# New DMA durations and stage priorities for the scheduler inside a two-branch attention kernel

## The chip, the cores and the metric

The kernel runs on one core of one Trainium2 chip. The metric is device time in microseconds from the first to the last instruction of the launch, as the median of several runs. The core has five instruction streams that run side by side and meet only through semaphores: TensorE (PE; its weight loads are listed apart as PEld), VectorE (DVE), ScalarE (ACT), GpSimd (POOL) and SyncE (SP). In this kernel SP does nothing but issue DMAs. The before kernel measures 364.31 us (three runs, 361.88 to 366.60); the profiled execution took 361.27 us, with a span of 359.5 us between first and last instruction.

## The reference

Two attention layers read the same input x (2048 tokens, width 640, 32 heads of 20) and their outputs are mixed by a per-token gate.

```python
# A: linear attention with a softmax feature map
q, k, v = split(x @ wqkv)                               # 32 heads of 20
phi = lambda t: concat(softmax(t @ w_phi), softmax(-(t @ w_phi)))
kv = einsum('bhsf,bhsd->bhfd', phi(k), v);  z = phi(k).sum(s)
a = ((phi(q) @ kv) / (phi(q) @ z + 1e-6)) @ wo
# B: four segments of 512 tokens: causal softmax attention inside the
#    segment plus a linear memory M, z carried over the segments
for s in range(4):
    p = softmax(q_s @ k_s.T * 20**-0.5 + causal);  dot = p @ v_s
    mem = (phi_B(q_s) @ M) / (phi_B(q_s) @ z + 1e-6)   # phi_B: t+1 if t>0 else exp(t)
    o_s = g * mem + (1 - g) * dot
    M += phi_B(k_s).T @ v_s;  z += phi_B(k_s).sum()
b = o @ wo
out = sigmoid(x . gate_w) * a + (1 - sigmoid(x . gate_w)) * b
```

## The kernel before

No order is written out by hand. The program describes some 1,490 operations as a graph (`op`, line 109, and `dma`, line 611). Each has the engines that may run it, an assumed duration, a priority `pr` (lower is sooner) and the tiles that it reads and writes. `schedule` (line 136) then plays the graph forward: at each step it takes, on every engine, the ready operation of lowest `pr` among those that could start within `DELTA` = 0.12 us of the earliest, and appends the one that starts first. For a DMA the assumed duration has two parts, `dur` (SP is occupied issuing) and `lat` (from the end of the issue to the landing). The result is one fixed list for each engine, with semaphore waits where lists depend on each other. The assumed times are used only to choose this order. On the chip every engine works through its list in that order, and an instruction that waits holds up all that stand behind it.

The names used below, with their lines:

- B works in 4 segments n of 8 steps g (four heads each), step number s = 8n + g, and this number is the common scale of all priorities. `b_step` (902) does the scores (QK, L923) in three bursts, the exponentials (L933, L952 on ACT), the causal masks (L938 on POOL) and the product with v (PV, L978 to L982). `combine` (988) divides, scales and writes `oB` on DVE, and so frees the PSUM banks of PV.
- `b_proj` (760) makes q and k (L782). Each head needs its 20 rows in its own quarter of the partitions, and 12 of the 32 rows in each quarter go elsewhere: four DMAs write them to DRAM ("relw", L790), four read them back ("relr", L793). Steps 5 to 7 of a segment need them.
- `b_mem` (830) updates the memory. It needs k with tokens on partitions, by five DMA transposes per segment ("kT", L838, tile `pk`); the first work on them is `pkt1` (L844, DVE).
- `a_k` (1052), for each of 16 token tiles t: the feature product and v (pkA and vA, L1065), exponentials, Zsum, Zrec and Anorm on DVE (L1080 to L1083), a DMA transpose of the result ("TT.t", issued through `spread`, L1097) and two adds of it into `acc` ("chain", L1090 and L1092).
- `a_kv` (1102): kv, 20 matmuls for each of two signs, once every four tiles (L1112); `a_fin` closes A's sums; `load_wo` loads the two output weights, 800 KB each ("WoA", "WoB").
- `a_q` (1155): Zq, rb, U (L1227) and the DMA transpose of the result ("oTA", L1242); `b_out` does the same for B ("oTB", L1040).
- `final` (1256): twenty matmuls per token tile against `Wo` (L1267, L1268), the eviction, and the store ("out", L1279).

PSUM has 8 banks, taken as 4 pairs; a score burst takes two pairs, so the next burst often waits for whoever must empty a pair. The constants that set the priorities stand at lines 495 to 509: `B0`, `V0`, `BN`, `VN` (projections), `KT`, `PK`, `MM` (memory), `PVP` (PV and combine), `OT`, `UO`, `AK`, `AQ`, `FI`. For example, TT and chain of tile t have priority `AK[0] + AK[1] * t`.

Of the kernel before, what the change touches and what calls it, by code (L numbers as in the profile page):

```python
# [13 lines left out]
D = 640  # L14
H = 32
DH = 20
NT = 16
NCH = 5
NG = 8
SEG = 4  # L20
LSEG = 512
HB = (0, 6, 12, 19, 24)
HEADS_OF = ((0, 6), (6, 12), (12, 19), (19, 25), (25, 31))
# [429 lines left out]
class GatedMix(Graph):  # L453
# [38 lines left out]
                if t.off < s.off + pool.size and s.off < t.off + t.size:  # L492
                    s.occ.append(t)

    B0 = (-10.0, 1.059)
    V0 = (-9.5, -0.512)
    BN = (-5.5, 0.604)
    VN = (-1.043, 0.3)
    PQ = (0.22, 1.0)
    KT = (2.0, 0.6)  # L500
    PK = (5.6, 0.3)
    MM = 6.815
    OT = (8.718, 0.2)
    PVP = (1.269, 1.394)
    FUQ = 3.0
    UO = (2.2, 0.6, 2.8)
    AK = (2.626, 1.032)
    AQ = (17.6, 4.1)
    FI = 10.953

    def memory(self):
        nc = self.nc
# [115 lines left out]
    def setup(self):  # L628
        ins = self.ins
        x2d = ins["A_x"].rearrange("b s d -> (b s) d")  # L630
        wqkv = ins["A_wqkv"]
        wsrc = lambda w: w.rearrange("(c p) n -> p c n", p=128)
        xT = self.xT
        def xload(s, pr, dur):
            sl = slice(LSEG * s, LSEG * (s + 1))
            return self.dma("sp", xT[:, :, sl], x2d[sl, :], W=[(xT, s)], pr=pr, transpose=True, name=f"x{s}", dur=dur, lat=3.0)
# [1 line left out]
        self.op("dve", 0.1, lambda e: e.memset(zf[:, :, :], 0.0), W=[(zf, "*")], pr=-60)  # L638
        self.op("act", 1.5, lambda e: e.activation(zf[:, :, :], zf[:, :, :], ACT.Exp), W=[(zf, "*")], pr=-60)
        xr = self.xr  # L640
        self.dma("sp", xr[:, :, :], x2d[0:LSEG, :].rearrange("(t p) d -> p t d", p=128), W=[(xr, "*")], pr=-60, lat=4.3, name="xr")
        for k, (st, w) in enumerate(((self.stq, "B_wq"), (self.stk, "B_wk"))):
            for h, (k0, k1) in enumerate(self.PIECES[k]):
                self.dma("sp", st[:, k0:k1, :], wsrc(ins[w])[:, k0:k1, :], W=[(st, h)], pr=-59 + 2 * k + 0.1 * h, dur=0.45, lat=5.0 + 2.6 * k + 0.25 * h, name="st")
        self.dma("sp", self.WvB[:, :, 0:D], wsrc(ins["B_wv"]), W=[(self.WvB, "w")], pr=-54, lat=8.0, name="WvB")
        self.dma("sp", self.wkT[:, :, :], wqkv[0:D, D:2 * D], W=[(self.wkT, "*")], pr=-53, dur=5.0, lat=7.0, transpose=True, name="wkT")
        self.dma("sp", self.WvA[:, :, :], wsrc(wqkv[:, 2 * D:3 * D]), W=[(self.WvA, "*")], pr=-52, lat=10.0, name="WvA")
        xload(1, -51, 4.0)
        xload(2, -50, 4.0)
        self.dma("sp", self.wqT[:, :, :], wqkv[0:D, 0:D], W=[(self.wqT, "*")], pr=-49, dur=5.0, lat=2.5, transpose=True, name="wqT")  # L650
        xload(3, -48, 4.0)
        self.dma("pool", self.WvB[:, :, D:D + 1], ins["gate_w"].rearrange("(c p o) -> p c o", p=128, o=1), W=[(self.WvB, "g")], pr=-40, lat=8.0, noncontig=True, name="gw")
        self.dma("pool", self.beta[:, :], ins["B_beta"].partition_broadcast(128), W=[(self.beta, "*")], pr=-38, lat=7.5, noncontig=True, name="beta")
        self.dma("pool", self.wphi[:, :, :], ins["A_w_phi"].rearrange("h d f -> (h d) f").rearrange("(c p) f -> p c f", p=128), W=[(self.wphi, "*")], pr=-39, lat=7.5, noncontig=True, name="wphi")
# [34 lines left out]
        for c in range(NCH):  # L689
            pt = self.pst("x0", 1)  # L690
# [7 lines left out]
        for w, st in ((0, self.stq), (1, self.stk)):  # L698
# [20 lines left out]
           W=[(Bs, "*")], pr=0)  # L719
        op("pool", 0.8, lambda e: e.affine_select(v, v, pattern=[[-1, 640]], compare_op=ALU.is_ge, fill=0.0, base=DH - 1, channel_multiplier=DH),  # L720
           W=[(Bs, "*")], pr=0)
        self.dma("sp", Bs[32:64, :, :], Bs[0:32, :, :], R=[(Bs, "*")], W=[(Bs, 1)], pr=0, name="Bsel")
        for k, (wT, Wd) in enumerate(((self.wkT, self.WkA), (self.wqT, self.WqA))):
            for ic in range(NCH):
                self.fuse(wT, Wd, ic, (0.0 if k == 0 else self.FUQ) + 0.1 * ic)
# [34 lines left out]
    def b_proj(self, n):  # L760
# [27 lines left out]
        prr = base + 5 * (self.BN[1] if n else self.B0[1])  # L788
        for i in range(4):
            self.dma("sp", scr.rearrange("(c s r) w t -> s r c (w t)", s=4, r=12)[i], qk[32 * i + DH:32 * i + 32, 0:5, :, :].rearrange("p c w t -> p c (w t)"),  # L790
                     R=[(qk, (w, c)) for w in range(2) for c in range(NCH)], W=[(sT, i)], pr=prr, nbytes=123e3, name="relw")
        for i in range(4):
            self.dma("sp", qk[32 * i:32 * i + DH, 5:8, :, :].rearrange("p c w t -> p c (w t)"), scr.rearrange("(m i d) w t -> i d m (w t)", i=4, m=3)[i],  # L793
                     R=[(sT, "*")], W=[(qk, f"r{i}")], pr=prr, nbytes=123e3, name="relr")
        for tl in range(4):
            t = 4 * n + tl
            pr = (self.V0[0] + self.V0[1] * tl) if n == 0 else 8 * n + self.VN[0] + self.VN[1] * tl
# [32 lines left out]
    def b_mem(self, n):  # L830
        if n >= SEG - 1:
            return
        qk = self.qk[n % 2]
        mp = self.pst("M", 2)
        vt = self.v1B[n % 2]
        pk = self.sbt("pk", [128, 4, D], BF16, self.p_pk)
        for c in range(NCH):
            self.dma("sp", lambda c=c: pk[:, :, 128 * c:128 * (c + 1)], qk[:, c, 1, :], R=[(qk, (1, c))],  # L838
                     W=[(pk, c)], pr=8 * n + self.KT[0] + self.KT[1] * c, transpose=True, dur=1.25, lat=1.9, name="kT")
        for tl in range(4):  # L840
            pr = 8 * n + self.PK[0] + self.PK[1] * tl
            tm = self.sbt("tmp", [128, D], BF16, self.p_tmp)
            rg = [(pk, c) for c in range(NCH)]
            self.op("dve", 0.36, lambda e, tl=tl, tm=tm: e.tensor_scalar(tm[:, :], pk[:, tl, :], 1.0, 1.0, op0=ALU.add, op1=ALU.max),  # L844
                    R=rg, W=[(tm, "*")], pr=pr, name="pkt1")
            self.op("act", d_act(D), lambda e, tl=tl: e.activation(pk[:, tl, :], pk[:, tl, :], ACT.Exp), R=[(tm, "*")],
                    W=[(pk, ("t", tl))], pr=pr, name="pkexp")
            self.op("dve", 0.56, lambda e, tl=tl, tm=tm: e.tensor_tensor(pk[:, tl, :], pk[:, tl, :], tm[:, :], ALU.min),
                    R=[(tm, "*")], W=[(pk, ("t", tl))], pr=pr, name="pkmin")
        pr = 8 * n + self.MM  # L850

        def mm(e):
            for c in range(NCH):
                b, c0 = (0, 168 * c) if c < 3 else (1, 168 * (c - 3))
                for k, h0 in enumerate((4 * c, XH[c])):
                    n4 = min(4, H - h0)
                    for tl in range(4):
                        r = e.matmul(self.pf(mp, b, c0 + 84 * k, 21 * n4), lhsT=pk[:, tl, 128 * c:128 * (c + 1)],
                                     rhs=vt[:, tl, h0:h0 + n4, :], start=(tl == 0), stop=(tl == 3))
            return r  # L860
        self.op("pe", 40 * 0.04, mm, R=[(pk, ("t", tl)) for tl in range(4)] + [(vt, tl) for tl in range(4)] + [(vt, "one")], W=[(mp, 0), (mp, 1)], pr=pr, name="Mmm")
        Mz = self.Mzb[n % 2]
        for b, c0, c1 in ((0, 0, 3), (1, 3, 5)):
            w = 168 * (c1 - c0) - (21 if c1 == 5 else 0)
            msl = self.M32[:, 168 * c0:168 * c0 + w]
            if n == 0:
                self.op("dve", d_dve(w, 1, True), lambda e, b=b, w=w, msl=msl: e.tensor_copy(msl, self.pf(mp, b, 0, w)),
                        W=[(mp, b), (self.M32, b)], pr=pr, name="Macc")
            else:
                self.op("dve", d_dve(w, 1, True), lambda e, b=b, w=w, msl=msl: e.tensor_tensor(msl, msl, self.pf(mp, b, 0, w), ALU.add),  # L870
                        W=[(mp, b), (self.M32, b)], pr=pr, name="Macc")
        self.op("dve", d_dve(819), lambda e: e.tensor_tensor(
            Mz[:, 0:819], self.M32[:, 0:819], self.Mm[:, 0:819], ALU.mult),
            R=[(self.M32, 0), (self.M32, 1), (self.Mm, "*")], W=[(Mz, "*")], pr=pr, name="Mz")
# [157 lines left out]
    def b_out(self, n):  # L1032
        oB = self.oB
        for qi in range(4):
# [2 lines left out]
            self.oTB[4 * n + qi] = oT  # L1037
            rd = [(oB, (g, qi // 2)) for g in range(NG)]
            if n < SEG - 1:
                self.dma("sp", lambda oT=oT: oT[:, :, :], lambda qi=qi: oB[:, qi, :], R=rd, W=[(oT, "*")], pr=pr, transpose=True, dur=1.28, lat=1.8, name="oTB")  # L1040
                continue
            pt = self.pst("oTB", 1)

# [52 lines left out]

    def spread(self, E, T, pr):  # L1097
        self.dma("sp", lambda: T[:, :, :], lambda: E[:, :, :].rearrange("p s n -> p (s n)"), R=[(E, 0), (E, 1)], W=[(T, 0), (T, 1)], pr=pr, transpose=True,
                 dur=1.34, lat=2.1, name="TT")
        return T  # L1100

    def a_kv(self, S):
        pr = self.AK[0] + self.AK[1] * (4 * S + 4)
        ts = [4 * S + i for i in range(4)]
        for s in range(2):
            pt = self.pst("kv", 2)

            def mm(e, s=s, pt=pt):
                for c in range(NCH):
                    b, c0 = (0, 160 * c) if c < 3 else (1, 160 * (c - 3))  # L1110
                    for k, t in enumerate(ts):
                        r = e.matmul(self.pf(pt, b, c0, 160), lhsT=self.Et[t][:, s, 128 * c:128 * (c + 1)],  # L1112
                                     rhs=self.vt[t][:, DH * HB[c]:DH * HB[c] + 160], start=(k == 0), stop=(k == 3))
                return r
            self.op("pe", 20 * 0.08, mm, R=[(self.Et[t], s) for t in ts] + [(self.vt[t], "*") for t in ts], W=[(pt, 0), (pt, 1)], pr=pr, name="kv")
            for b, c0, c1 in ((0, 0, 3), (1, 3, 5)):
# [38 lines left out]
    def a_q(self, S):  # L1155
# [57 lines left out]
        for tl in range(4):  # L1213
# [26 lines left out]
            oT = self.sbt("oTA", [128, NCH, 128], BF16, self.p_oTA)  # L1240
            if S < SEG - 1:
                self.dma("sp", lambda oT=oT: oT[:, :, :], lambda oA=oA: oA[:, :], R=[(oA, 0), (oA, 1)], W=[(oT, "*")], pr=pru + 0.5,  # L1242
                         transpose=True, dur=1.28, lat=1.8, name="oTA")
            else:
                pt = self.pst("oTA", 1)

# [9 lines left out]
    def final(self, t):  # L1256
# [19 lines left out]
            self.op("pe", d_mm(*[512, 128] * 10), part(0, 10), R=[(oA, "*"), (oB, "*"), (self.Wo, 0), (self.Wo, 1)], W=P, claim=[ob], pr=pr, name="final")  # L1276
        self.evac(640, lambda: ob[:, :], lambda: self.pf(pt, 0, 0, 640), W=[(pt, 0), (pt, 1), (ob, "*")], pr=pr, name="out_ev")
        out2d = self.out.rearrange("b s d -> (b s) d")
        self.dma("sp", out2d[128 * t:128 * (t + 1), :], lambda: ob[:, :], R=[(ob, "*")], pr=pr, nbytes=164e3, name="out")  # L1279

    def build_all(self):
        self.Et, self.vt, self.oTB, self.oTA, self.TTs, self.phiT = {}, {}, {}, {}, [], {}
# [71 lines left out]
```

## Time and profile before

| what | value |
|---|---|
| time, median of 3 (range) | 364.31 us (361.88 to 366.60) |
| profiled span, granted TensorE clock | 359.5 us, 0.957 |
| ACT, POOL busy | 262.5 us (73%), 109.6 us (30%) |
| DMA: packets, bytes | 68,823, 27.52 MB (60,400 packets under 512 B) |
| issue to landing, median: TT, kT, oTB, oTA | 3.3, 2.8, 2.7, 3.4 us |

Idle time of an engine counts only where that engine, or one that waits for it, sets the pace. So the stages have to be told apart: up to about 40 us loading and first projections, from 40 to about 200 us B's segments 0 to 2 beside A's keys, from 200 us on B's segments 2 and 3 beside A's queries and the output product, and from about 340 us the last outputs alone.

### The profile page before, as it was taken

The numbers are of one execution on the slowest core, as the hardware profiler recorded it, in microseconds if no ns is written. First come the engines' busy times: TensorE is split into PE (matmuls) and PEld (weight loads), VectorE is DVE, ScalarE is ACT, GpSimd is POOL, SyncE is SP. The second block draws the span as 40 slices with busy tenths as digits, with TensorE's granted clock in tenths as the row PEclk, the third lists the DMA queues.
The fourth block names the chain that finished last, engine by engine and source line by source line (L and its number), as shares of the span: only waits on it lengthen the run. The fifth ranks groups of instructions, "written<-read, shape, count | busy, mean of one in ns | idle before, by whom it ended". The sixth has DMA issues, their size and how long they took to land.

```text
span 359.5 us, 8970 instructions
## 1 busy us (share of the span) xinstructions
PE 313.9 (87%) x3824; PEld 180.8 (50%) x3824; DVE 244.4 (68%) x479; ACT 262.5 (73%) x362; POOL 109.6 (30%) x170
## 2 busy tenths in 40 slices
PE   3999759898999799779995899979999998888896
PEld 2454424456555444565544455545556454454663
DVE  5625557798699999899995979234782439455560
ACT  3569758894999798868995898628887779166721
POOL 7832203422223435324242323202221223131400
PEclk9999969999999999998998999989999999699699
DMA  7999741364323516742238002851014202132001
GB/s 202 246 237 184 123 82 36 57 107 88 46 38 75 90 24 91 137 69 38 38 98 178 3 2 37 122 104 52 2 38 105 64 20 17 22 57 57 2 20 55
DMA packets 68823, 27.52 MB, mean 77 GB/s; under 512 B 60400, under 2 KB 66864, under 8 KB 68784
## 3 DMA queue, kind: packets, MB, share of 16 engines
q1 hardware_dynamic: 68688, 26.92, 39.2%
q8 instruction: 30, 0.49, 0.6%
q0 software_dynamic: 96, 0.04, 0.3%
q14 instruction: 9, 0.07, 0.1%
HBM read 7.57 MB, written 4.59 MB: 34 GB/s over the span
## 4 chain that ended last, share of the span: by engine, by line
PE 45%; DVE 28%; ACT 15%; DMA 6%; SPq 2%; issue 2%; POOL 1%
PE ps L1267 11%; ACT expT L933 8%; PE ps L978 5%; PE ps L782 5%; PE ps L1166 5%; DVE E L1083 5%; DMA TT<-E 4%; DVE z L1080 4%; PE ps L923 3%; DVE acc L1092 3%; PE ps L1268 3%; PE ps L803 2%; ACT expT L952 2%; PE ps L769 2%; DVE cb L1024 2%; PE ps L1227 2%
## 5 line engine op out<-in xcount | busy, mean ns | idle before, releaser
L938 POOL TENSOR_SCALAR_AFFINE_SELECT expT<-expT 128x512 bf16<-128x512 bf16 x128 | 91.2, 714 | 226.9 <-ACT expT L933 166.3
L933 ACT ACTIVATE expT<-ps 128x1024 bf16<-128x1024 f32 x128 | 123.4, 1027 | 12.6 <-PE ps L923 12.2
L923 PE MATMUL ps<-qk 20*128 20x512 bf16 (+3 forms) x512 | 35.5, 310 | 17.3 <-DVE oB L1019 6.3
L782 PE MATMUL ps<-xT,WB 128*128 128x512 bf16 x175 | 44.4, 387 | 3.5 <-DVE oB L1019 2.0
L978 PE MATMUL ps<-v1B,expT 128*128 128x21 bf16 x1280 | 43.4, 174 | 4.0 <-POOL expT L938 1.6
L978 PEld LDWEIGHTS ps<-v1B,expT 128*128 128x128 bf16 x1280 | 39.5, 97 | 13.2 <-POOL expT L938 3.7
L752 ACT ACTIVATE out<-ps 128x640 bf16<-128x640 f32 x16 | 11.3, 703 | 37.8 <-PE ps L1268 37.8
L952 ACT ACTIVATE expT<-ps 128x1024 bf16<-128x1024 f32 x32 | 32.7, 1022 | 5.5 <-PE ps L923 5.4
L923 PEld LDWEIGHTS ps<-qk 20*128 20x128 bf16 x512 | 10.3, 92 | 42.8 <-issue 8.9
L1267 PE MATMUL ps<-Wo,oTA 128*128 128x512 bf16 x80 | 25.9, 410 | 5.4 <-DMA oTA<-oA 2.7
L1171 ACT ACTIVATE ET<-ps 128x512 bf16<-128x512 f32 x40 | 23.1, 606 | 4.7 <-PE ps L1166 4.4
L1166 PE MATMUL ps<-xT,WqA 128*128 128x512 bf16 x100 | 24.8, 382 | 1.4 <-ACT expT L952 1.1
L782 PEld LDWEIGHTS ps<-xT,WB 128*128 128x128 bf16 x175 | 15.0, 98 | 21.4 <-DVE oB L1019 2.7
L1065 PE MATMUL ps<-WvA,xT 128*128 128x512 bf16 x80 | 24.9, 398 | 0.8 <-ACT expT L933 0.4
L1267 PE MATMUL ps<-Wo,oTB 128*128 128x512 bf16 x80 | 25.1, 399 | 0.0
L1083 DVE TENSOR_TENSOR E<-E,z 128x1280 bf16<-128x1280 bf16 x16 | 24.2, 1515 | 0.5
L1080 DVE TENSOR_REDUCE z<-E 128x64 f32<-128x1280 bf16 x16 | 23.6, 1477 | 1.0 <-ACT E L1072 1.0
L1065 PE MATMUL ps<-WkA,xT 128*128 128x512 bf16 x80 | 23.5, 380 | 0.6 <-ACT expT L933 0.5
L803 PE MATMUL ps<-WvB,xT 128*128 128x512 bf16 x80 | 23.8, 380 | 0.0
L1072 ACT ACTIVATE E<-ps 128x640 bf16<-128x640 f32 x32 | 22.7, 709 | 1.5 <-PE ps L1066 1.1
L1092 DVE TENSOR_TENSOR acc<-acc,TT 128x640 bf16<-128x640 bf16 x31 | 17.8, 573 | 8.5 <-DMA TT<-E 7.8
L1002 DVE TENSOR_TENSOR cs<-ps,epsv 128x32 f32<-128x32 f32 x24 | 4.5, 186 | 25.0 <-PE ps L982 24.9
(129 smaller groups left out, 586.8 us busy)
## 6 DMA issues: line engine op xcount, KB each, us to landing
out_dram<-out SPq DMA_DIRECT2D x16, 160.0 KB, 1.9
scr<-qk SPq DMA_DIRECT2D x16, 120.0 KB
qk<-scr SPq DMA_DIRECT2D x16, 120.0 KB
stq<-in_B_wq_dram SPq DMA_DIRECT2D x5, 160.0 KB
WvB<-in_B_wv_dram SPq DMA_DIRECT2D x1, 800.0 KB, 10.1
WvA<-in_A_wqkv_dram SPq DMA_DIRECT2D x1, 800.0 KB, 5.2
Wo<-in_A_wo_dram SPq DMA_DIRECT2D x1, 800.0 KB
Wo<-in_B_wo_dram SPq DMA_DIRECT2D x1, 800.0 KB
```

The lines of the kernel that those rows point to most:

```text
L782: r = e.matmul(self.pf(pt, 0, 0, LSEG), lhsT=self.WB[:, w, kc, 128 * c:128 * (c + 1)], rhs=xT[:, kc, LSEG * n:LSEG * (n + 1)], start=(kc = ...
L803: e.matmul(self.pf(pt, 0, 0, 512), lhsT=l, rhs=self.WvB[:, kc, 0:512], start=(kc == 0), stop=(kc == 4))
L923: r = e.matmul(self.pf(pts[i][0], pts[i][1], c0, N), lhsT=qk[32 * i:32 * i + DH, g, 1, 128 * j:128 * (j + 1)], rhs=qk[32 * i:32 * i + DH, ...
L933: self.op("act", d_act(1024), lambda e, p=p, pt=pt: e.activation(ex[:, 2 * p:2 * p + 2, off:off + 512], self.pbanks(pt, 0, 2, 512), ACT.Ex ...
L938: self.op("pool", d_pool(n_el), lambda e: e.affine_select(view(), view(), pattern=pat, compare_op=ALU.is_ge, fill=0.0, base=0, channel_mul ...
L952: return e.activation(ex[:, :, 1024:1280].rearrange("p (k b) c -> p k b c", k=2), src, ACT.Exp, scale=scale)
L978: r = e.matmul(self.pf(ad, b, 84 * q2 + 21 * i, 21) if n else self.pf(ad, 0, 84 * qi + 21 * i, 21), lhsT=ex[:, i, c0:c0 + 128], rhs=vt[:, ...
L1065: e.matmul(self.pf(pt, 0, 0, 512), lhsT=l, rhs=W[:, kc, 0:512], start=(kc == 0), stop=(kc == 4))
L1080: self.op("dve", 1.42, lambda e: e.tensor_reduce(rz[:, :], Ev(), axis=AX.X, op=ALU.add), R=[(E, 0), (E, 1)], W=[(rz, "*")], pr=pr, name="Z ...
L1083: self.op("dve", d_dve(1280), lambda e: e.tensor_tensor(Ev(), Ev(), rz[:, :].rearrange("p (h o) -> p h o", o=1).to_broadcast([128, 2 * H, ...
L1166: r = e.matmul(self.pf(pt, 0, 0, LSEG), lhsT=self.WqA[:, kc, 128 * c:128 * (c + 1)], rhs=xT[:, kc, LSEG * S:LSEG * (S + 1)], start=(kc == ...
L1267: e.matmul(self.pf(pt, 0, 0, 512), lhsT=l, rhs=self.Wo[:, c, 0:512], start=(c == 0), stop=(c == 9))
```

## The change

The scheduler's picture of the DMAs is brought to what a trace shows (issue and landing times of the first loads, of the relocation, of the transposes and stores), the priorities are chosen anew on that picture, and the kv matmuls take the exact width of each group of heads (140 columns for seven heads, 160 for eight) in place of 160 for all.

```diff
-    B0 = (-10.0, 1.059)
-    V0 = (-9.5, -0.512)
-    BN = (-5.5, 0.604)
-    VN = (-1.043, 0.3)
+    B0 = (-10.536, 1.059)
+    V0 = (-8.527, -0.104)
+    BN = (-5.724, 0.604)
+    VN = (-1.043, 0.457)
     PQ = (0.22, 1.0)
-    KT = (2.0, 0.6)
-    PK = (5.6, 0.3)
-    MM = 6.815
-    OT = (8.718, 0.2)
-    PVP = (1.269, 1.394)
-    FUQ = 3.0
+    KT = (2.0, 0.662)
+    PK = (5.993, 0.3)
+    MM = 6.776
+    OT = (9.192, 0.582)
+    PVP = (1.403, 1.394)
+    FUQ = 3.206
     UO = (2.2, 0.6, 2.8)
-    AK = (2.626, 1.032)
-    AQ = (17.6, 4.1)
-    FI = 10.953
+    AK = (2.575, 1.021)
+    AQ = (17.6, 4.075)
+    FI = 10.254
...
 # first loads, assumed times only (wkT as an example; xr, st, WvB, WvA, x1 to x3, wqT likewise)
-        ... pr=-53, dur=5.0, lat=7.0, transpose=True, name="wkT")
+        ... pr=-53, dur=9.9, lat=2.1, transpose=True, name="wkT")
...
 # relocation
-        ... W=[(sT, i)], pr=prr, nbytes=123e3, name="relw")
+        ... W=[(sT, i)], pr=prr, dur=0.9, lat=4.3, name="relw")
-        ... W=[(qk, f"r{i}")], pr=prr, nbytes=123e3, name="relr")
+        ... W=[(qk, f"r{i}")], pr=prr, dur=0.36, lat=2.6, name="relr")
...
 # transposes and stores
-        ... transpose=True, dur=1.25, lat=1.9, name="kT")
+        ... transpose=True, dur=(1.27 if n else 1.7), lat=2.0, name="kT")
-        ... dur=1.34, lat=2.1, name="TT")
+        ... dur=1.36, lat=2.5, name="TT")
-        ... dur=1.28, lat=1.8, name="oTB")     # oTA the same
+        ... dur=1.28, lat=2.2, name="oTB")     # oTA the same
-        ... ob[:, :], R=[(ob, "*")], pr=pr, nbytes=164e3, name="out")
+        ... ob[:, :], R=[(ob, "*")], pr=pr, dur=0.42, lat=2.0, name="out")
...
 # a_kv
+                    lo, w = HEADS_OF[c][0], DH * (HEADS_OF[c][1] - HEADS_OF[c][0] + 1)
                     for k, t in enumerate(ts):
-                        r = e.matmul(self.pf(pt, b, c0, 160), lhsT=self.Et[t][:, s, 128 * c:128 * (c + 1)],
-                                     rhs=self.vt[t][:, DH * HB[c]:DH * HB[c] + 160], start=(k == 0), stop=(k == 3))
+                        r = e.matmul(self.pf(pt, b, c0 + DH * (lo - HB[c]), w), lhsT=self.Et[t][:, s, 128 * c:128 * (c + 1)],
+                                     rhs=self.vt[t][:, DH * lo:DH * lo + w], start=(k == 0), stop=(k == 3))
```

The number of operations stays the same. What moves is their place in the five lists. The stretches of SP's list (DMA issues) and of DVE's list that matter most, read from the two built programs (`a.0` is the first of its kind, `..` a run of them):

```
SP, first segment
  before: relw.0..3 Bsel kT.0 kT.1 relr.0..3 kT.2 kT.3 kT.4 TT.0 | TT.1 TT.2 relw.4..7 relr.4..7 TT.3
  after:  relw.0..3 Bsel kT.0 kT.1 relr.0..3 TT.0 kT.2 kT.3 kT.4 | TT.1 relw.4 TT.2 relw.5..7 TT.3 relr.4..7
SP, third segment's relocation, then the output weights
  before: TT.9 relw.8..11 relr.8..11 TT.10 kT.10..12 TT.11 ... TT.13 oTB.4 WoA TT.14 WoB TT.15
  after:  TT.9 relw.8..11 TT.10 relr.8..11 kT.10 kT.11 TT.11 ... TT.13 oTB.4 WoA WoB TT.14 TT.15
SP, fourth segment's relocation
  before: oTA.0 relw.12 relw.13 oTA.1 relw.14 relw.15 oTB.5 out.0 relr.12 relr.13 oTA.2 oTB.6 out.1 relr.14
  after:  relw.12..15 oTA.0 relr.12..15 oTA.1 oTB.5 out.0 oTA.2 oTB.6 out.1
DVE, first segment
  before: fuse_ev.8 pkt1.0 combine(0,0) chain.0 chain.1 pqmin.1 pkmin.0 pkt1.1 combine(0,1)
  after:  fuse_ev.8 pqmin.1 pqt1.2 qk_ev.15 pqmin.2 fuse_ev.9 chain.0 combine(0,0) chain.1 combine(0,1)
          Zsum.1 Zrec.1 Anorm.1 pkt1.0
PE, first segment
  before: PV(0,0) QK(0,1) third burst, pkA.1, QK(0,2) first burst, PV(0,1)
  after:  one q/k projection more, QK(0,1) third burst, pkA.1, PV(0,0), QK(0,2) first burst, PV(0,1),
          QK(0,2) second burst, the next q/k projection
```

## The prediction

> **What bounds the kernel now.** I read the page first, then busy time by stage, then who waited for whom, and last the order of time around the largest waits. The page says that TensorE is busy for 313.9 of 359.5 us and nothing else comes near:
>
> ```profile
> PE 313.9 (87%) x3824; PEld 180.8 (50%) x3824; DVE 244.4 (68%) x479; ACT 262.5 (73%) x362; POOL 109.6 (30%) x170
> ```
>
> The shares by stage (seven stretches that I cut where the kind of work changes) say something else:
>
> ```profile
> core 0: us, PE busy (x) PEld busy (x) DVE busy (x) ACT busy (x) POOL busy (x), PEclk, DMA share, GB/s
> 0.00:40.00 40.00, 33.96 (x243) 17.74 (x244) 22.05 (x48) 26.04 (x44) 21.65 (x47) 1.00 0.97 207
> 40.00:100.00 60.00, 50.37 (x605) 27.95 (x602) 42.36 (x75) 45.19 (x64) 16.03 (x22) 0.94 0.43 73
> 100.00:190.00 90.00, 79.85 (x1079) 46.81 (x1078) 85.12 (x146) 79.21 (x104) 33.62 (x42) 0.98 0.42 72
> 190.00:200.00 10.00, 6.35 (x50) 4.39 (x49) 6.73 (x15) 4.49 (x8) 1.90 (x3) 0.83 0.48 135
> 200.00:300.00 100.00, 93.75 (x1208) 52.69 (x1207) 58.16 (x133) 77.69 (x110) 24.51 (x38) 0.98 0.26 49
> ```
>
> From 100 to 190 us VectorE is the full engine (85.1 of 90) and TensorE has 10 us to spare; from 200 us on TensorE is full (93.8 of 100). Between 40 and 200 us TensorE idles 9.6 + 10.2 + 3.6 = 23.4 us, although VectorE also idles from 40 to 100 us. So there is an early stretch in which both stand, and VectorE works it off later. The waits name the cause:
>
> ```profile
> PE ps L923 <- DVE oB L1019: 6.3, 1, 6.3
> PE ps L1267 <- DMA oTA<-oA: 2.7, 1, 2.7
> DVE tmp L844 <- DMA pk<-qk: 8.2, 2, 6.9
> DVE acc L1092 <- DMA TT<-E: 7.8, 4, 3.2
> ```
>
> In order of time around 42 us:
>
> ```profile
> 42.67 3.82 SPq L614 DMA_TRANSPOSE pk<-qk  x3
> 46.53 1.43 SPq L614 DMA_TRANSPOSE TT<-E  x1
> 47.90 0.33 DVE L844 TENSOR_SCALAR tmp<-pk 128x640 bf16<-128x640 bf16 x1 [6.88 <-DMA pk<-qk]
> 49.19 0.61 PE L923 MATMUL ps<-qk 20*128 20x512 bf16 x4 [6.27 <-DVE oB L1019]
> 50.44 0.33 DVE L1090 COPY acc<-TT 128x640 bf16<-128x640 bf16 x1 [1.31 <-DMA TT<-E]
> ```
>
> The planner had put `pkt1.0` ahead of combine(0,0). Its operand lands at 47.9 us, behind it stand the instructions that free the PSUM pair, and TensorE's next score burst waits 6.27 us for that pair. Two smaller holes of the same kind:
>
> ```profile
> 184.62 0.54 SPq L619 DMA_DIRECT2D Wo<-in_A_wo_dram  x1
> 185.32 1.36 SPq L614 DMA_TRANSPOSE TT<-E  x1
> 186.73 0.81 SPq L619 DMA_DIRECT2D Wo<-in_B_wo_dram  x1
> 192.12 1.02 DVE L1092 TENSOR_TENSOR acc<-acc,TT 128x640 bf16<-128x640 bf16 x2 [3.22 <-DMA TT<-E]
> ...
> 235.68 0.59 PE L1267 MATMUL ps<-Wo,oTA 128*128 128x512 bf16 x1 [2.65 <-DMA oTA<-oA]
> ```
>
> TT.14 takes 6.8 us (185.32 to 192.12) where the median is 3.3, with one 800 KB load ahead of it and one behind. final.2 waits for oTA.2, which SP issued only at 232.17, after a relr that had to wait for the relocation to land.
>
> VectorE's waits for DMAs from 40 to 200 us add up to 6.88 + 1.31 + 1.68 (TT.1) + 1.55 (TT.3) + 1.37 (kT.5 to kT.9) + 1.32 (TT.10) + 3.22 = 17.3 us.
>
> [...] combine(0,0) was ready and stood 6.88 us behind pkt1.0. [...] The kv groups show 1.56 us for 20 pairs, 78 ns at 160 columns.
>
> **The change part by part.**
>
> *First segment (TT.0 and pkt1.0).* SP's times up to 42.67 us should stay: it is busy from 5.8 to 35.7 us with the same loads in the same order. TT.0 now goes at 42.67; before, it landed 50.42 - 46.53 = 3.9 us after its issue, so about 46.6. VectorE was free for pkt1.0 at 41.0 and now has about 2 us more in front (an 0.8 us eviction and four short products), so chain.0 waits 46.6 - 43.0 = 3.6 us in place of 6.88 + 1.31 = 8.2. combine(0,0) ends near 47.9 (0.3 us for chain.0, then 0.25 + 0.2 + 0.5). TensorE now has ahead of the first instruction that needs it: one projection (1.24 us), a score burst (0.4), PV(0,1) (1.2) and another burst (0.4), 3.2 us in all. Before, it resumed at 49.19 without these. Gain: 49.2 - 47.9 + 3.2 = 4.5 us (3 if the extra bursts wait for ScalarE). pkt1.0 itself now waits for nothing: its operand lands 1.4 us later than before, about 49.3, and 0.9 + 3.5 us of combine(0,1) and tile 1's norm stand in front.
>
> *The other transposes.* For each TT I add up, from the rows' mean durations, the VectorE work between Anorm.t and the chain that needs it; less than about 3.35 us makes a wait. Before: 1.4 us for TT.1, which gives the 1.68 us wait that the trace shows. After: 2.6 for TT.1 (0.7 us wait), 2.6 for TT.9 (0.8), 3.0 for TT.12 (0.4), 1.8 for TT.13 (1.5). TT.3 and TT.10 are no longer behind relr, 0.3 in place of 2.9. The kT of segment 1 costs 0.5 in place of 1.4. Sum apart from TT.0 and TT.14: 4.2 against 5.9 us. VectorE is full there, so this is worth its difference, 1.7 us; I take 1.5.
>
> *The output weights.* TT.14 now stands behind both loads, 1.6 MB. At the 0.25 MB per us that the page's best slices reach these take 6.5 us from about the time vA.15 ends, so TT.14 lands some 10 us after combine(1,7). VectorE has a vA eviction and a product more in front of chain.28, 8.2 us after combine(1,7) in place of 5.6. Wait: 2 us in place of 3.2, with 0 and 5 us as ends. I take a gain of 1.
>
> *Fourth relocation.* relr.12 comes before oTA.1 and no longer between out.0 and oTA.2. out.0 still does, and it waits for final.0's eviction. TensorE has final.1 (2.8), a burst (0.4), PV (1.2) and U.3 (0.8) between U.2 and final.2, 5.2 us, against 1.5 us for VectorE's part and 3.4 us for the transpose. Wait of 0.6 us in place of 2.65: gain 2.
>
> *kv width.* Of 160 pairs, 128 lose 20 columns: at most 128 x 8 ns = 1.1 us, at least nothing since the weight load of the pair stays (20 loads in 1.36 us). I take 0.5.
>
> *Everything else* is reordering without a reason in this trace: the other priorities and which engine evicts (VectorE has one operation more and ScalarE one less; their neighbours hide it). TensorE's holes of 0.4 us and more after 235 us sum to about 7 us, and a new order may make some and close some. I set 2.5 us against the gain, for new waits.
>
> Sum: 4.5 + 1.5 + 1 + 2 + 0.5 - 2.5 = 7.0, hence 364.3 - 7.0 = 357.3 us.
>
> **The rivals.**
>
> *Moved waits.* The head's gain is spent again because VectorE is full from 100 to 190 us with the same 85 us of work, and TT.13 and TT.14 (1.6 MB ahead) cost more. Then the head gives 2, the relocation 2, kv nothing, less 2: 362. For it: the planner's Wo loads keep their old assumed time, so their contention is still not seen. Against: VectorE's early waits are what fills it later.
>
> *New starvation, slower.* SP's list now has waits for VectorE inside both relocations (TT.2 between relw.4 and relw.5; TT.10 before relr.8). If a norm is late, steps 5 to 7 of a segment wait for their rows. With TT.14 at the 5 us end, a 3 us wait at relr, and 4 us in a tail where U.12 and U.13 come later: 364.3 + 2 + 3 + 4 - 4.5 = 369. Against: relr.4 is read a segment later, and relr.8 several steps later.
>
> *All holes close.* VectorE's 17.3 us shrink to 6, and TensorE's hole at 151 us (1.4 us, for Anorm.11 behind TT.10) goes too: 4.5 + 6 + 2 + 1 = 13.5, 351.
>
> **How the numbers follow.** Forecast (354 to 360.5) 0.57, moved waits (360.5 to 366) 0.24, starvation (over 366) 0.10, all holes close (under 354) 0.09. The forecast is the likeliest, 357.3. Two per cent is 7.3 us, so faster begins below 357.0, in the middle of the forecast: 0.09 + 0.37 = 0.46. Slower begins above 371.6: 0.06. Between: 0.48. The range 351.5 to 366.0 leaves out about 0.05 below and 0.10 above.
>
> **What would show it.** The first score burst of step 2 before 46 us, TensorE's hole at 43 us under 2 us, and chain.0 as VectorE's longest DMA wait there; DMA waits of VectorE from 40 to 200 us near 10 us; chain.28 still waiting 2 us or more; final.2 without its hole; kv pairs at 70 to 78 ns. It is wrong if TensorE's idle time before 200 us does not fall by some 5 us, or if relr or the tail has a new hole over 3 us.

## The result, and the profile after

| | before | after |
|---|---|---|
| time, median of 4 runs (range) | 365.46 us (361.88 to 369.55) | 348.28 us (346.74 to 349.84) |
| ratio to before, 95% interval | | 0.9561 [0.9463, 0.9660] |
| profiled span, granted TensorE clock | 359.5 us, 0.957 | 345.6 us, 0.965 |

Before has one run more here than in the table above. Some executions of a list take some 2% longer at a lower clock (kv_only below: 361.08 us at 0.961, 369.77 at 0.930); a ratio and its interval leave them out (here the 369.55 us of before), medians and ranges do not. The forecast was 357.3 us with a range of 351.5 to 366.0. The kernel is 9 us faster than that and lies below the range. TensorE is still the full engine, and its busy time has hardly changed:

```profile
PE 309.6 (90%) x3824; PEld 180.0 (52%) x3824; DVE 243.0 (70%) x480; ACT 262.5 (76%) x361; POOL 107.0 (31%) x170
```

Busy time by stage, cut as in the prediction (columns: PE, PEld, DVE, ACT, POOL, then granted clock, DMA share and GB/s):

```profile
40.00:100.00 60.00, 53.96 (x704) 30.58 (x705) 48.78 (x89) 51.40 (x70) 19.16 (x26) 0.94 0.48 73
100.00:190.00 90.00, 78.93 (x1004) 46.55 (x1001) 79.78 (x138) 75.37 (x102) 28.31 (x38) 0.96 0.48 87
190.00:200.00 10.00, 9.58 (x100) 4.83 (x100) 8.07 (x19) 6.08 (x9) 1.90 (x3) 0.83 0.01 2
200.00:300.00 100.00, 94.82 (x1260) 54.63 (x1252) 62.45 (x141) 81.14 (x113) 26.70 (x42) 1.00 0.30 51
```

VectorE does 6.4 us more between 40 and 100 us (48.8 against 42.4) and 5.3 us less between 100 and 190 us, where it was full. TensorE's idle time from 40 to 200 us falls from 23.4 to 6.0 + 11.1 + 0.4 = 17.5 us. The waits that carried the prediction:

```profile
PE ps L782 <- DVE oB L1019: 2.3, 1, 2.3
PE ps L1113 <- DVE cb L1024: 3.5, 2, 2.9
DVE acc L1092 <- DMA TT<-E: 5.0, 6, 2.3
DVE acc L1090 <- DMA TT<-E: 2.9, 1, 2.9
```

The wait for `pk` (8.2 us) and the one for `oTA` at final.2 (2.7 us) are gone. VectorE waits 5.0 + 2.9 = 7.9 us for DMAs between 40 and 200 us, against 17.3. In order of time around 42 us:

```profile
42.54 1.68 SPq L614 DMA_TRANSPOSE TT<-E  x1
...
45.70 0.39 PE L923 MATMUL ps<-qk 20*128 20x512 bf16 x4
...
48.48 0.48 DVE L1090 COPY acc<-TT 128x640 bf16<-128x640 bf16 x1 [2.86 <-DMA TT<-E]
...
49.92 2.31 PE L782 MATMUL ps<-xT,WB 128*128 128x512 bf16 x5 [2.30 <-DVE oB L1019]
```

TT.0 goes where the prediction put it, and the score burst of step 2 starts at 45.70 us. But TT.0 takes 5.9 us to land instead of 3.9, so chain.0 still stops VectorE, and TensorE still has a hole, 2.30 us instead of 6.27. That is a favourable trace: in seven other kernels below whose lists are the same here (no_kv, wo_late, hole_back, late_old, late_old_d, late_far, late_long_d) this hole is 2.6 to 4.8 us.

The time is not won there alone. I cut the trace at the end of the last kv matmul (197.94 us before, 191.61 after). In both kernels the late part then holds the same TensorE work. Each part is split in three: TensorE idle; the time that a halved TensorE clock cost (estimated as half of TensorE's busy time inside each stretch in which the record shows a granted clock of 0.50); and the rest, which is TensorE's work at full clock. Such a stretch about halves the pace: before's last kv group lies in one and takes 2.85 us, where the others take 1.54 to 1.56, and the matmuls of 512 columns of L1065 start 0.53 us apart in one (at 53 us) and 0.27 us apart outside (at 42 us).

| us | before, early | after, early | before, late | after, late |
|---|---|---|---|---|
| length | 197.9 | 191.6 | 161.6 | 154.0 |
| TensorE idle | 29.5 | 24.7 | 16.2 | 11.4 |
| lost to the half clock | 6.1 | 6.1 | 7.4 | 4.5 |
| rest | 162.4 | 160.8 | 137.9 | 138.1 |

So 6.3 us were won early (4.8 idle, 1.6 work) and 7.6 us late (4.8 idle, 2.9 half clock). The prediction had expected the late part to stay as it was (2 us from the relocation less 2.5 for new waits).

This is one trace of each, and the two halves are not equally sure. Seven more traces follow after's lists up to the end of kv, apart from one move in SP's list in wo_late, and end kv between 189.3 and 196.0 us; three more follow before's lists (kv_only, ota2_early, late_new) and end it between 198.2 and 204.4. So the early gain is there, but 6.3 us is one draw. The late part repeats better: 153.4 and 153.7 us in no_kv and wo_late, which have after's late lists, and 162.6 and 162.0 in kv_only and head_only, which have before's. The cut also splits the half clock unevenly: a stretch of 3.4 us ends with the cut in before (194.56 to 197.97) and begins just behind it in after (192.01 to 195.43), and each costs some 1.7 us.

The windows of the two late parts, before first, give the same length and idle time (length less PE busy):

```profile
197.94:359.51 161.57, 145.39 (x1870) 84.67 (x1867) 90.10 (x201) 108.39 (x147) 36.38 (x56) 0.95 0.23 43
```

```profile
191.61:345.64 154.03, 142.64 (x1873) 84.89 (x1873) 92.64 (x208) 110.14 (x148) 36.40 (x57) 0.97 0.24 45
```

### The profile page after: what moved, and what is told of

It is laid out like the page before. It is cut to its first block, busy times and chain, and to the rows that moved or that the text cites. A ratio compares the mean times of both kernels' runs of the same rounds, so it can differ in the third digit from the quotient of the medians.

```text
span 345.6 us, 8962 instructions
## 1 busy us (share of the span) xinstructions
PE 309.6 (90%) x3824; PEld 180.0 (52%) x3824; DVE 243.0 (70%) x480; ACT 262.5 (76%) x361; POOL 107.0 (31%) x170
## 4 chain that ended last, share of the span: by engine, by line
PE 53%; DVE 19%; ACT 17%; DMA 9%; issue 1%; POOL 1%
PE ps L1268 9%; ACT expT L933 8%; DMA TT<-E 8%; PE ps L782 6%; PE ps L1065 6%; PE ps L978 6%; PE ps L1167 4%; PE ps L923 3%; PE ps L803 3%; PE ps L1228 3%; DVE acc L1092 2%; DVE E L1083 2%; PE ps L1269 2%; ACT expT L952 2%; PE ps L769 2%; DVE cb L1024 2%
## 5 line engine op out<-in xcount | busy, mean ns | idle before, releaser
L938 POOL TENSOR_SCALAR_AFFINE_SELECT expT<-expT 128x512 bf16<-128x512 bf16 x128 | 88.4, 692 | 214.7 <-ACT expT L933 156.4
L978 PE MATMUL ps<-v1B,expT 128*128 128x21 bf16 x1280 | 42.9, 173 | 5.8 <-DVE vA L753 1.8
L923 PE MATMUL ps<-qk 20*128 20x128 bf16 (+3 forms) x512 | 35.1, 307 | 7.4 <-ACT expT L933 1.5
L1167 PE MATMUL ps<-xT,WqA 128*128 128x512 bf16 x100 | 26.1, 400 | 0.4 <-ACT ET L1172 0.2
L1065 PE MATMUL ps<-WvA,xT 128*128 128x512 bf16 x80 | 26.1, 412 | 0.1
L1268 PE MATMUL ps<-Wo,oTA 128*128 128x512 bf16 x80 | 23.5, 380 | 1.8 <-ACT expT L933 1.2
L1065 PE MATMUL ps<-WkA,xT 128*128 128x512 bf16 x80 | 23.5, 381 | 1.0 <-DVE KVZacc L1124 0.6
L1268 PE MATMUL ps<-Wo,oTB 128*128 128x512 bf16 x80 | 23.5, 380 | 0.0
L1092 DVE TENSOR_TENSOR acc<-acc,TT 128x640 bf16<-128x640 bf16 x31 | 17.0, 548 | 5.5 <-DMA TT<-E 5.0
```

The lines of the kernel that those rows point to most:

```text
L923: r = e.matmul(self.pf(pts[i][0], pts[i][1], c0, N), lhsT=qk[32 * i:32 * i + DH, g, 1, 128 * j:128 * (j + 1)], rhs=qk[32 * i:32 * i + DH, ...
L938: self.op("pool", d_pool(n_el), lambda e: e.affine_select(view(), view(), pattern=pat, compare_op=ALU.is_ge, fill=0.0, base=0, channel_mul ...
L978: r = e.matmul(self.pf(ad, b, 84 * q2 + 21 * i, 21) if n else self.pf(ad, 0, 84 * qi + 21 * i, 21), lhsT=ex[:, i, c0:c0 + 128], rhs=vt[:, ...
L1065: e.matmul(self.pf(pt, 0, 0, 512), lhsT=l, rhs=W[:, kc, 0:512], start=(kc == 0), stop=(kc == 4))
L1092: self.op("dve", 0.5, lambda e, h=h: e.tensor_tensor(acc[:, :, :], acc[:, :, :], T2[:, :, 64 * h:64 * h + 64], ALU.add), R=[(T2, 0), (T2, ...
L1167: r = e.matmul(self.pf(pt, 0, 0, LSEG), lhsT=self.WqA[:, kc, 128 * c:128 * (c + 1)], rhs=xT[:, kc, LSEG * S:LSEG * (S + 1)], start=(kc == ...
```

## The experiments

Lists are moved by hand in some kernels. A small helper, called after `schedule()`, takes operations out of their engine's list and puts them behind a named one; all dependencies stay. `cmbp.0` is combine(0,0), `cmbp.1` combine(0,1). All other times come from the scheduler as the diff says. The kernels ran in four groups, each beside its own runs of before (medians 363.71, 365.30, 365.91 and 367.34 us). Differences of kernels of one group are the safest; between groups absolute times hold to about 1%, which is why the traces are read there too.

**First group: which part carries the gain.** Starting from before, the kv widths alone, the new durations alone, and the new priorities alone.

```diff
 # kv_only, on before (the lists stay)
-                        r = e.matmul(self.pf(pt, b, c0, 160), ...
-                                     rhs=self.vt[t][:, DH * HB[c]:DH * HB[c] + 160], ...
+                        r = e.matmul(self.pf(pt, b, c0 + DH * (lo - HB[c]), w), ...
+                                     rhs=self.vt[t][:, DH * lo:DH * lo + w], ...
 # times_only, on before: every dur= and lat= of the change, old priorities, old kv
-        ... W=[(sT, i)], pr=prr, nbytes=123e3, name="relw")
+        ... W=[(sT, i)], pr=prr, dur=0.9, lat=4.3, name="relw")
...
 # prio_only, on before: every constant of the change, old durations, old kv
-    OT = (8.718, 0.2)
+    OT = (9.192, 0.582)
...
```

> The kernel before with the exact kv widths and nothing else; every list keeps its order. Columns alone: 128 matmuls lose 20 columns, 128 x 8 ns, so at most 1.1 us less, and L1112's pairs, which take 84 ns in the kernel before (13.45 us for 160), come to about 77. Rival: the width sets the pace of the pair more strongly, since in the changed kernel the pairs took 67 ns (10.73 us for 160); then up to 2.7 us less. Both inside the noise of the whole time: within 1% of before.

> The kernel before with the new DMA durations alone: old priorities, old kv widths. If the gain comes from the planner's knowledge of the DMAs, most of it is here: 349 to 355 us. Its VectorE list even has combine(0,0) ahead of chain.0, so the hole at 43 us should be gone. If the new priorities bring it, this kernel is within 1% of before.

> The kernel before with the new priorities alone: old DMA durations, old kv widths. In its VectorE list pkt1.0, chain.0 and pkmin.0 all stand ahead of combine(0,0), so the hole at 43 us should be longer than 6.3 us (up to 10). If the durations bring the gain: no faster than before, 362 to 370 us. If the priorities bring it: under 356 us in spite of that hole.

And once more, later, the change without its kv widths:

```diff
 # no_kv, on after (the lists stay)
-                        r = e.matmul(self.pf(pt, b, c0 + DH * (lo - HB[c]), w), ...
+                        r = e.matmul(self.pf(pt, b, c0, 160), ...
...
```

> The changed kernel with the old kv width of 160 columns; all lists the same. The pairs took 69 ns at 160 and 61 ns at 140 columns in the runs so far, 1.1 us for 128 of them. TensorE is not the full engine where kv.0 to kv.5 stand: 0 to 1.1 us more than the changed kernel. If the gain of the whole needs the widths, over 2 us more.

| kernel | priorities | durations | kv | median us | ratio to before, 95% |
|---|---|---|---|---|---|
| kv_only | old | old | exact | 367.48 | 1.0046 [0.9995, 1.0097] |
| times_only | old | new | 160 | 372.77 | 1.0171 [0.9989, 1.0354] |
| prio_only | new | old | 160 | 366.95 | 1.0119 [1.0005, 1.0234] |
| no_kv | new | new | 160 | 346.46 | 0.9453 [0.9408, 0.9497] |
| after | new | new | exact | 348.28 | 0.9561 [0.9463, 0.9660] |

Neither half is faster alone, and both together are 4 to 5% faster. In times_only the score burst comes early, but new holes of 4.95 us (at 48.2) and 4.14 us (at 197.0) open; the trace is of a run of 373.47 us, so their sizes are rough. In prio_only the hole at the start of segment 1 grows to 7.49 us and one of 4.79 us opens at 201 us. The priorities belong to the durations on which they were chosen. The kv widths do shorten TensorE's early work (162.4 us in no_kv as in before, 160.8 in after), but neither pair shows a gain in time. A likely reason is that the work saved lies where TensorE waits anyway: its early idle time is 22.4 us in no_kv and 24.7 in after.

**The output weights ahead of TT.14** (run with the first group).

```diff
 # wo_late, on after, SP's list
+        self.move(["WoA.0", "WoB.0"], "TT.15")
```

> The changed kernel with one move in SP's list: both 800 KB loads of the output weights are issued after TT.14 and TT.15; all other lists are untouched. If TT.14's landing behind these loads makes the hole at 187 us (TensorE 2.9 us, VectorE 2.3 us), TT.14 lands 3.4 to 4 us after its issue, the hole falls under 1 us, and the half-rate clock stretch after it may go too: 1.5 to 4 us less than the changed kernel. If chain.28 waits for another reason, no change.

Measured: 344.24 us, 0.9471 [0.9390, 0.9552]. First the stretch in after, then in wo_late:

```profile
178.12 0.52 SPq L619 DMA_DIRECT2D Wo<-in_B_wo_dram  x1
180.22 6.66 SPq L614 DMA_TRANSPOSE TT<-E  x2
185.52 1.41 PE L1113 MATMUL ps<-vA,E 128*128 128x140 bf16 x20
187.53 1.02 DVE L1092 TENSOR_TENSOR acc<-acc,TT 128x640 bf16<-128x640 bf16 x2 [2.34 <-DMA TT<-E]
```

```profile
180.50 6.34 SPq L614 DMA_TRANSPOSE TT<-E  x2
185.40 1.01 DVE L1092 TENSOR_TENSOR acc<-acc,TT 128x640 bf16<-128x640 bf16 x2
188.05 1.42 PE L1113 MATMUL ps<-vA,E 128*128 128x140 bf16 x20 [0.50 <-DVE cb L1024]
```

With both loads behind TT.15, chain.28 no longer waits, and TensorE's hole ahead of the second kv batch falls from 2.93 to 0.50 us. In the seven other traces with the loads ahead of TT.14 as in after (no_kv, chain0_late and the five kernels on after of the late part) chain.28 waits 2.2 to 2.8 us, and the hole is 1.1 to 3.7 us. So the wait came from the loads, which the planner's fixed durations can't tell. In the traces wo_late is 4.1 us ahead of after at final.0 and 2.5 us at the end. In time its gain over after is not shown by this run alone: the two intervals overlap, and no_kv, with the loads ahead, has much the same ratio. It shows in both_late below.

**The head alone, and the fourth relocation alone** (second group, on before).

```diff
 # head_only, on before: DVE's list, and the exponential of the same tile on ACT
+        self.move(["pkt1.0"], "cmbp.0")
+        self.move(["pkexp.0"], "exp.9")
 # ota2_early, on before: SP's list
+        self.move(["oTA.2"], "oTB.5")
```

> The kernel before with two moves: pkt1.0 behind combine(0,0) in VectorE's list, pkexp.0 behind the exponentials of step 2's first burst in ScalarE's. TensorE then has a burst, PV(0,1), a q/k projection and vA.1 (4.3 us) ahead of the first instruction that needs pkt1.0. If the hole at 43 us costs what it lasts, the hole shrinks from 6.3 to about 2 us, the half-rate stretch after it may shrink with it, and the run takes 4 to 6 us less than before. If the head's gain is spent again because VectorE is full from 100 to 190 us, the milestones come back to those of before by 190 us and the run is within 1 us of before.

> The kernel before with one move in SP's list: oTA.2 is issued right behind oTB.5, ahead of out.0 and of the relr that waits. Idle time alone: the hole ahead of final.2 falls from 2.65 to about 0.6 us, 2 us less than before. If a hole also costs the half-rate stretch that follows it (3.4 us at half clock at 235.5 us in the kernel before), 3 to 4 us less. If later stages absorb it, no change.

head_only: 367.77 us, 1.0130 [1.0095, 1.0166], no gain but a small loss. combine(0,0) ends at 42.9 us, 6.3 us sooner than in before, and yet combine(0,1) ends 1.2 us later:

```profile
49.65 0.33 DVE L844 TENSOR_SCALAR tmp<-pk 128x640 bf16<-128x640 bf16 x1 [6.76 <-DMA pk<-qk]
51.39 0.40 PE L923 MATMUL ps<-qk 20*128 20x384 bf16 x8 [4.18 <-ACT E L1072]
52.11 0.33 DVE L1090 COPY acc<-TT 128x640 bf16<-128x640 bf16 x1 [2.14 <-DMA TT<-E]
54.89 1.46 PE L782 MATMUL ps<-xT,WB 128*128 128x512 bf16 x3 [3.11 <-DVE oB L1019]
```

VectorE stands 6.76 us all the same, one operation further on, and one hole of 6.27 us has become two of 4.18 and 3.11. Moving `pkt1.0` by one place is not enough: it still stands ahead of combine(0,1), and TT.0, issued behind three kT, holds VectorE for 2.14 us more ahead of it. The change moved both. Whether VectorE's order alone would do, with `pkt1.0` and chain.0 behind combine(0,1), was not tried.

ota2_early: 362.78 us, 0.9874 [0.9785, 0.9964], a small gain at most, and 356.4 us in the trace against 359.5 (runs of one list differ by more than that, so only the stretch itself is read here). The hole ahead of final.2 only shrank, from 2.65 to 1.98 us, since oTA.2 was issued just 1.2 us sooner:

```profile
230.98 1.28 SPq L614 DMA_TRANSPOSE oTA<-oA  x1
```

Still 2.3 us were won between final.0 and final.3, 0.7 of them at the hole and 1.6 behind it. What went with it is the stretch of half clock that begins at the hole in before; the trace of ota2_early has none from 198.9 to 304.7 us. The stretch in before, then the same matmuls of final.2 in before and in ota2_early:

```profile
235.50:238.91 3.41, 3.23 (x13) 1.61 (x14) 0.38 (x1) 0.00 (x0) 0.00 (x0) 0.50 0.64 162
236.16 0.63 PE L1267 MATMUL ps<-Wo,oTA 128*128 128x512 bf16 x1
```

```profile
235.66 0.38 PE L1267 MATMUL ps<-Wo,oTA 128*128 128x512 bf16 x1
```

**The wait that the change left at the head** (second group, on after), and then both moves together.

```diff
 # chain0_late, on after: DVE's list
+        self.move(["chain.0", "chain.1"], "cmbp.1")
 # both_late, on after: this and wo_late
+        self.move(["chain.0", "chain.1"], "cmbp.1")
+        self.move(["WoA.0", "WoB.0"], "TT.15")
```

> The changed kernel with chain.0 and chain.1 moved behind combine(0,1) in VectorE's list, so that TT.0's landing holds up neither combine. TensorE's hole of 2.3 us at 47.6 us should go, and VectorE's wait of 2.9 us shrinks little. If holes carry through to the end: 2 to 4 us less than the changed kernel (with the half-rate stretch at 48.65 us). If the tight VectorE stage absorbs it: no change.

> chain0_late and wo_late together. If the two gains are independent, about 4 us (measured for wo_late) plus whatever chain0_late gives less than the changed kernel: 340 to 343 us. If one is spent in the other, 344 us.

chain0_late: 345.08 us, 0.9417 [0.9340, 0.9495]. VectorE waits for TT.0 about as long as in after, but both combines are done by then, and the projection comes without its hole. Part of the hole moves on: TensorE stops 5 us later for an eviction that stands behind chain.0, chain.1 and the norm of tile 1.

```profile
46.53 1.03 PE L782 MATMUL ps<-xT,WB 128*128 128x512 bf16 x4 [0.16 <-DVE cs L1013]
...
49.65 0.61 DVE L1090 COPY acc<-TT 128x640 bf16<-128x640 bf16 x1 [2.67 <-DMA TT<-E]
...
55.28 0.29 PE L923 MATMUL ps<-qk 20*128 20x256 bf16 x4 [3.49 <-DVE qk L753]
```

combine(0,1) ends 4.3 us sooner than in after; 2.2 us of this are left at the first kv and 2.4 at the end. both_late: 339.81 us (337.75 to 343.37), 0.9270 [0.9204, 0.9335], the fastest kernel of the study. It is faster than chain0_late, though the intervals almost meet, and clearly faster than after. Its trace, of the run of 343.37 us, is 5.8 us ahead of after at the end of kv and 4.0 us at the end. Of VectorE's DMA waits there is left, beside 0.7 us at chain.0:

```profile
DVE acc L1092 <- DMA TT<-E: 1.9, 5, 0.6
```

**The late part** (third and fourth group). Since over half of the trace's gain lay there, I took the constants and durations that only the late part reads, forward on before and back on after.

```diff
 # late_new, on before (third group)
+    OT = (9.192, 0.582)
+    AQ = (17.6, 4.075)
+    FI = 10.254
+        ... dur=1.28, lat=2.2, name="oTB")     # oTA the same
+        ... dur=0.42, lat=2.0, name="out")
 # late_old, on after (third group)
+    OT = (8.718, 0.2)
+    AQ = (17.6, 4.1)
+    FI = 10.953
 # late_old_d, on after (third group)
+        ... dur=1.28, lat=1.8, name="oTB")     # oTA the same
+        ... nbytes=164e3, name="out")
 # late_long_d, on after (fourth group)
+        ... dur=1.28, lat=2.6, name="oTB")     # oTA the same
 # late_far, on after (fourth group): as far again past the new values
+    OT = (9.666, 0.964)
+    AQ = (17.6, 4.05)
+    FI = 9.555
 # hole_back, on after (fourth group): SP's list, the hole ahead of final.2 put back
+        self.move(["oTA.2"], "out.1")
```

> The kernel before with the new values of what acts late: priorities OT, AQ, FI and the durations of oTA, oTB and the stores. Its lists are those of before up to final.2 (entry 237 of 364 on TensorE). The changed kernel gained some 7 us between the end of kv.7 and the end. If these late values bring that gain by themselves, this kernel takes 4 to 7 us less than before. If the gain needs the whole plan, or is the tail that happens to follow the new early part, it is within 2 us of before, or slower.

> The changed kernel with the old priorities OT, AQ, FI; lists unchanged up to entry 282 of 364 on TensorE (final.5). If the late gain is the new priorities, 2 to 5 us more than the changed kernel. If the durations or the early part bring it, within 1 us.

> The changed kernel with the old durations of oTA, oTB and the stores (issue to landing 0.4 us shorter for the transposes); its lists are those of the changed kernel up to entry 274 of 364 on TensorE. If knowing these landings closes the late holes, finals wait for oTA again: 2 to 5 us more than the changed kernel, with holes ahead of final.8 to final.11. If not, within 1 us of it.

> The changed kernel with the landings of oTA and oTB assumed 0.4 us longer than measured (2.6 after the issue in place of 2.2), the mirror of late_old_d, which assumed them 0.4 us shorter and took about 4 us more. If knowing the landing matters, a longer assumption costs little: no DMA wait ahead of a final, within 2 us of the changed kernel. If any change to a plan whose priorities were chosen for it costs, this one costs 3 to 6 us too, without a DMA wait.

> The changed kernel with OT, AQ and FI moved by the same amounts past the new values, the mirror of late_old (about 4 us more). If the new values are better because of their direction, this is within 2 us of the changed kernel or faster. If the values are a tuned point, 2 to 6 us more.

> The changed kernel with oTA.2 issued behind out.1 in SP's list, which puts the hole ahead of final.2 back: some 2 us by the sum of eviction, issue and landing less the work between. Hole alone: 2 us more than the changed kernel at final.3 and at the end. Hole and a half-rate stretch after it: 3.5 to 4 us more. Absorbed later: less than 1 us at the end.

late_new measures 376.33 us, 1.0175 [1.0067, 1.0282]: these values on the old plan are slower, and the hole ahead of final.2 is still there (2.80 us). The others, with the late part of each trace split as above (all have 137.9 to 139.8 us of work in it); medians are of the runs that a ratio counts:

| kernel | median us (runs) | late part | idle | half clock |
|---|---|---|---|---|
| before | 364.31 (3) | 161.6 | 16.2 | 7.4 |
| after | 348.28 (4) | 154.0 | 11.4 | 4.5 |
| no_kv (third group) | 346.46 (4) | 153.4 | 11.5 | 3.3 |
| late_old (third) | 349.73 (2) | 156.3 | 12.1 | 6.1 |
| late_old_d (third) | 351.42 (3) | 159.0 | 14.4 | 5.4 |
| late_far (fourth) | 347.56 (4) | 153.4 | 11.1 | 3.4 |
| hole_back (fourth) | 351.40 (4) | 158.1 | 13.9 | 5.5 |
| late_long_d (fourth) | 351.35 (1) | 160.4 | 15.7 | 4.9 |

Beside no_kv of the same group, which has the lists of after, going back on the late priorities costs about 3 us (in the late part of the trace 2.9; the two runs, 347.52 and 351.93, lie far apart), and going back on the late durations about 5 us (5.6 in the trace, of a run of 356.71 us). Assuming too long a landing costs 7.0 us of the late part beside late_far of its group, and 3.8 us in its one run that counts; the other three took 356.65 to 359.49. Priorities past the new ones cost nothing. With the shorter landing of late_old_d a wait for a transpose comes back (in late_long_d none does, and its late part is longer still):

```profile
264.55 0.38 PE L1268 MATMUL ps<-Wo,oTA 128*128 128x512 bf16 x1 [1.37 <-DMA oTA<-oA]
```

hole_back measures by itself what the prediction had priced at its idle time:

```profile
229.44 1.20 SPq L614 DMA_TRANSPOSE oTA<-oA  x1
...
232.06 0.61 PE L1268 MATMUL ps<-Wo,oTA 128*128 128x512 bf16 x1 [2.27 <-DMA oTA<-oA]
```

```profile
231.28:234.69 3.41, 2.63 (x10) 1.26 (x11) 1.23 (x3) 0.00 (x0) 0.00 (x0) 0.50 0.05 9
```

A hole of 2.27 us comes back, with 3.41 us at half clock that begin inside it; TensorE is busy for 2.63 us of these, so they cost 1.3. The late part is 4.1 us longer than in after, and the median is 3.8 us above late_far of the same group. Hole and stretch make 3.6 us of this: here a hole cost clearly more than its length.

## Why the prediction was wrong, point by point

*First segment* (4.5 us): the mechanism held, the size was a little less. chain.0 is VectorE's longest wait for a DMA, 2.86 us against 3.6, but this is near by luck: two terms were off and cancel in part. TT.0's landing, "about 46.6", became about 48.4. And VectorE came to chain.0 at 45.62 and not at 43.0: `fuse_ev.8` ended at 42.54, 1.5 us later than in before, and two further evictions stood behind it, where the prediction had counted one eviction in all. Why TT.0 took 5.9 us is not separated: it had the relocation's reads ahead of it and three kT behind. combine(0,0) ended at 49.86 and not "near 47.9", and a hole of 2.30 us stayed. At the first kv 3.4 us were won. head_only shows that VectorE's order must change by more than one place, and the trace of chain0_late that about 2 us more lay in the wait left.

*The other transposes* (1.5 us): VectorE's DMA waits were put near 10 us in all and are 7.9; apart from chain.0 and chain.28 they are 2.7 us, against 4.2 forecast and 5.9 in before. The direction was right and the waits fell further; what that was worth in time was not isolated.

*The output weights* (1 us): chain.28 was to wait 2 us and waits 2.34. Right, and wo_late shows that the cause given, both loads ahead of the transpose, is the cause of this wait.

*kv width* (0.5 us): by the prediction's own measure, 20 matmuls take 1.41 us, 70.5 ns each, against 78, inside its 70 to 78. The 8 ns for 20 columns were an estimate, and hold: in after's trace one matmul takes 225 ns at 140 columns and 233 at 160 (means). In time no gain can be seen: no_kv is not slower than after.

These four were to give 7.5 us before the end of kv; 6.3 came in this pair of traces.

*Fourth relocation* (2 us): the hole ahead of final.2 closed whole, 2.65 us. But the price was only the idle time. hole_back and ota2_early show that the clock goes with it, and hole_back puts such a hole at about 4 us.

*Everything else* (-2.5 us) is the step that failed: "I set 2.5 us against the gain, for new waits". (The holes after 235 us, which the prediction put at about 7 us, add up to 6.2.) In the late part TensorE's idle time fell by 4.8 us, of which the relocation is 2.65: the rest was to grow by 2.5 and fell by 2.1. Its holes of 0.4 us and more went from 10.0 to 4.1 us in all. And no term of the sum knew the half clock, which cost 2.9 us less in the late part; some 1.6 us of that lie at the relocation's hole. Together: 0.7 more from the relocation, 4.6 from the holes, 2.9 from the clock, 8.1 us, less the 1.2 us that the first four missed. That is the 6.9 us between the forecast gain of 7.0 and the 13.9 us of the traces. The early terms of this sum move with the trace that one takes, the late ones hold in those that repeat the late part.

The argument of the prediction, that a new order makes some holes and closes some, treated the late part as a shuffle. The runs back from it (late_old, late_old_d, late_long_d, hole_back) are all slower, late_far isn't: of the neighbours tried, those with another assumed landing or with the old priorities are worse. That the late gain comes from landing times that hold on the chip is not shown: late_long_d assumes a longer landing, has no wait for a transpose and still loses. It fits as well that priorities chosen for one set of durations lose with any other. What stays open is why each single neighbour loses: apart from hole_back it is many holes under 1.7 us at different places, and I can name only those for oTA.

Of the rivals, "all holes close" at 351 us was nearest, but for a reason that it didn't have: VectorE's waits did shrink to 7.9, yet over half of the trace's gain is in the late part, of which it had only the relocation. "Moved waits" was right that the contention of the output weights is unseen by the planner, and wrong that the gain would be spent again. The starvation that "new starvation" feared isn't in the trace: no TensorE hole of 1 us or more between 40 and 200 us waits for a DMA (VectorE and ScalarE end them all), and no hole after 235 us is longer than 1.34 us.

## What to carry to other kernels

Durations and priorities of a planner are one setting: tune them together, and judge neither by a run with the other left old. Price a TensorE hole such as the one of 2.27 us here at its length plus the half-rate clock that may follow (1.3 us there), and count what the new plan does in the stage that TensorE fills, not only at the waits that one can name. Where the planner can't know a thing, such as a transpose behind a large load, moving one entry by hand after it has planned is cheap: two such moves gave 4 us more in the trace and 8 us in the medians. And read a stage from more than one trace: kernels with the same lists ended the same stage 189 to 196 us into the span.

## What the runs showed of the hardware

- In these traces TensorE's granted clock falls to 0.50 for 3.41 us or 6.83 us at a time: 30.7 us of before's span and 23.9 of after's. Five of before's six such stretches begin inside a hole of 1.1 to 6.3 us or within 0.8 us of its end. Of after's four, two begin inside a hole, one 1.8 us behind one, and one (at 137.40) has only a hole of 0.6 us ahead of it. In after a hole of 1.34 us (at 321.56) was followed by 6.83 us at half rate, while one of 1.78 us (at 179.97) had none right behind it. In no_kv the same hole, 1.79 us at 179.13, was followed by 3.41 us at half rate. In these traces the length of a hole alone does not decide what follows it.
- The same list varies in time, and its clock with it: the 23 runs of before in the first group had spans from 357.7 to 367.4 us, and the longer ones had the lower mean clock (correlation -0.74, about 3.4 us for each 0.01). By estimate a loss of 0.01 over 362 us is 3.6 us by itself, so the clock can account for the slope; that it is the cause was not tested. The medians, 362.0 us at 0.952 and 346.6 at 0.9655, lose 17.4 and 12.0 us in this way (span times one less the clock), which would make some 5 us of the gain clock. This counts idle TensorE time too and so is an upper figure; by busy time the two traces give 2.9 us.
- A transpose of 164 KB from SBUF to SBUF (TT, 128x640 bf16; median from issue to landing 3.3 us in before, 3.7 in after) took 5.9 us, up to the add that waited for it, between the relocation's reads and three more transposes (5.1 to 7.0 us over ten kernels with this order) and 7.3 us behind the 1.6 MB of output weights (7.2 to 7.8 over the eight with that order).
